# A transformer block on one core: the first Q operand on GpSimd's queue, eight more matmuls ahead of the maxima, the last K and Q parted on GpSimd, and four smaller moves

## The chip, the core and the metric

The kernel runs on one core of one Trainium2 chip. The metric is the device time of one execution in microseconds. TensorE (PE) multiplies, VectorE (DVE), ScalarE (ACT) and GpSimd (POOL) do the elementwise work, and DMAs are issued from the queues of SP, ACT and POOL. The engines run their own instructions in order and wait for each other through semaphores.

## The reference

All arrays are float32. 2048 rows of width 512 go through attention with 32 heads of 16 and a gated feed-forward part of width 1792; both are modulated by a vector `c`.

```python
mod = (_silu(c) @ w_mod).reshape(1, 6, 1, -1)
sa, ca, ga, sb, cb, gb = (mod[:, i] for i in range(6))
h = layernorm(x) * (1 + ca) + sa
q, k, v = heads(h @ wqkv)                        # 32 heads of 16
o = softmax(q @ k.T * 16 ** -0.5) @ v
x = x + ga * (merge(o) @ wo)
h = layernorm(x) * (1 + cb) + sb
x = x + gb * ((silu(h @ w_gate) * (h @ w_up)) @ w_down)
```

## The kernel before

**Numbers in two parts.** A matmul operand is held as a high part (rounded to the form that TensorE multiplies, by a cast) and a low part (what the cast left out, by a subtraction). A product takes three matmuls: high by high, high by low, low by high (`mm3`, line 205). So each operand costs a cast, mostly on ScalarE, and a subtraction, on VectorE or GpSimd.

**The ramp (lines 229 to 355).** While x and the first weights land, VectorE makes the statistics of the first 512 rows. The modulation by `sa` and `ca` is made in two halves: `mod_part` multiplies a half of `w_mod` by silu(c) into bank 7 and copies it to `ev`, `mod_col` turns it with TensorE transposes, and `half_prep` applies it to the turned rows: two casts on ScalarE, two subtractions on VectorE (line 349). In `half_prep(0, ...)` the copy of the second half's `ev` is done on VectorE (line 285, called at 347), ahead of those subtractions. `split_w` parts a block of `wqkv`: cast on ScalarE, subtraction on GpSimd (line 203).

**The projections (lines 392 to 472).** The rows are handled in four chunks of 512 (`ci`). `proj_T(ci, w, m)` gives 128 columns of Q or K, transposed: 12 matmuls into a bank, then a cast to `prt[:, 0]` (399), a subtraction out of the bank into `prt[:, 1]` (401), and two stores to the DRAM arrays `qd` and `kd` on SP's queue (404, 405). `prt` has four buffers. `proj_v` gives V for 128 rows. `Stream.jobs` writes the matmuls out one by one; every third of them advances the posts, that is, the next of the steps that follow a job. A lane is other work with a period: the lane "m" takes a step every 7 matmuls, from the second chunk on, and runs `mods()`.

**The modulation weights (lines 298 to 313 and 369 to 390).** For each of the other four sixths of `w_mod` (called 4, 3, 2 and 5) `mod_sum` multiplies four slices by silu(c) on GpSimd (line 300, one scalar operand) and adds them up (301, 302); a matmul with ones then sums over the partitions (307 for columns, 312 for rows). The weights are staged in three buffers that they share with the blocks of `wqkv`. The loads are issued on SP where `load(v)` stands: 4 and 3 at the start, 2 behind the sum of 4, 5 behind that of 3.

**The last K and Q beside the first maxima (lines 887 to 950).** The softmax needs the row maxima of the scores ahead of the scores. `max_one` (501) makes a 128 x 512 piece of scores on TensorE (line 510) and VectorE takes its maximum (512). A unit is four heads by 512 rows, with 64 such pieces in 16 steps of four; the maxima run 21 steps (`LEAD`) ahead of the scores. The generator `late` holds the projections that are left: K and Q of chunk 3, two of chunk 2, and eight of V, 216 matmuls. 22 of them come first (`take(late, 22)`); then each six maxima are followed by 14. Projections use banks in turn (`bank`), maxima others (`four`): banks 4, 5, 6 ahead of the maxima, and from there on 4 and 5, with 0, 1, 2, 3, 6, 7 for the maxima. `load_q(u)` and `load_k(u)` read a unit's Q and K from `qd` and `kd`, in two halves each; for the first three units all halves go over SP's queue, later the second halves over POOL's.

**The main loop.** Scores (line 557), exponentials (559) and the products with V (572) run unit by unit (32 of them), with maxima of the unit ahead; from the second quarter on the output projection and the feed-forward part of the finished chunk are worked in between ("filled" stretches), those without are called plain. When a unit ends, `close_unit` (894) reads the row sums back as `dn` (583), and at the steps `i0 + 3`, `+ 4`, `+ 5` come the reciprocal on VectorE (587) with its store (588), the broadcast back `rb` (593), and the multiply on GpSimd (599) with its store. `i0` is two steps behind the end, or none for a chunk's last unit. In the feed-forward part GpSimd also parts the products `mid` (832, 833), and SP loads weights (703, 708).

Of the kernel before, what the change touches and what calls it, by code (L numbers as in the profile page):

```python
# [9 lines left out]
F32 = mybir.dt.float32  # L10
# [4 lines left out]
ALU = mybir.AluOpType  # L15
# [4 lines left out]
P = 128  # L20
# [8 lines left out]
CW = S // NC  # L29
NG = H // 4  # L30
# [8 lines left out]
KR = 48  # L39
# [20 lines left out]
def take(it, k):  # L60
    run(islice(it, k))
# [40 lines left out]
def block_kernel(ctx, tc, x, wqkv, wo, w_gate, w_up, w_down, c, w_mod, out):  # L102
    nc = tc.nc
# [6 lines left out]
    sm = Stream()  # L110
# [14 lines left out]
    minus = const.tile([P, P], F32, name="minus")  # L125
    eps_t = const.tile([P, 1], F32, name="eps_t")
    one = const.tile([P, 1], F32, name="one")
    modc = const.tile([P, 4, NK], F32, name="modc")
    gb_bc = const.tile([P, D], F32, name="gb_bc")

# [141 lines left out]
        nc.tensor.matmul(banks[i % 4][:, 0:2 * P], busy[:, 0:P], busy[:, 0:2 * P], start=True, stop=True)  # L272
    nc.vector.memset(eps_t, EPS)
    nc.vector.memset(one, 1.0)
    sc = pa.tile([P, NK], F32, name="sc")
    nc.scalar.activation(sc, c_sb, AF.Silu)
    nc.scalar.activation(pa.tile([P, 1], F32, name="warm0"), eps_t, AF.Sqrt)

    def mod_part(wm, copy=nc.scalar.copy):
        pb_ = single("pmod")  # L280
        for k in range(NK):
            nc.tensor.matmul(pb_[32 * k:32 * k + 32, :], sc[:, k:k + 1].to_broadcast([P, 32]), wm[:, k, :],
                             start=True, stop=True)
        ev = pa.tile([P, D], F32, name="ev", tag="ev", bufs=1)
        copy(ev, pb_)
        return ev
# [10 lines left out]

    def mod_sum(wm):
        for k in range(NK):
            nc.gpsimd.tensor_scalar_mul(wm[:, k, :], wm[:, k, :], sc[:, k:k + 1])  # L300
        nc.gpsimd.tensor_add(wm[:, 0:2, :], wm[:, 0:2, :], wm[:, 2:4, :])
        nc.gpsimd.tensor_add(wm[:, 0, :], wm[:, 0, :], wm[:, 1, :])

# [6 lines left out]
    def sum_row(wm, dst, factor):  # L310
        pr_ = single("prow")
        nc.tensor.matmul(pr_, one.to_broadcast([P, P]), wm[:, 0, :], start=True, stop=True)
        nc.scalar.mul(dst, pr_, factor)

    def split_w(src, c0, eng=nc.gpsimd):
        cols = slice(c0, c0 + P)
        split(wqs[0][:, :, cols], wqs[1][:, :, cols], src, eng)
# [21 lines left out]
    def half_prep(ab, ev):  # L339
        mod_col(ev, half_cols(ab))  # L340
        if ab == 0:
            turn_two(2)
        tps = tps0[2 * ab:2 * ab + 2]
        lows = [modulate(pa, hT[0], tps[e], 0, 2 * ab + e, e, False) for e in range(2)]
        for _, h32, high in lows:
            nc.scalar.copy(high.bitcast(F32R), h32)
        nxt = mod_part(wm_ab[1], nc.vector.tensor_copy) if ab == 0 else None
        for low in lows:
            nc.vector.tensor_sub(*low)
        return nxt  # L350
# [1 line left out]
    bank = Turn(4, 5, 6, 7)  # L352
    turn_two(0)
    ev = half_prep(0, ev)
    split_w(wst0[:, 1], 0)

    def weights():
        st_ = {}
# [10 lines left out]
    def mods():  # L369
        def load(v):  # L370
            w = load_mod(v)
            mod_sum(w)
            return w

        def ticks(k):
            for _ in range(k):
                yield

        w4, w3 = load(4), load(3)
        yield from ticks(9)  # L380
        sum_col(w4, modc[:, 2, :], 1.0)
        w2 = load(2)
        yield from ticks(4)
        sum_col(w3, modc[:, 3, :], 0.0)
        w5 = load(5)
        yield from ticks(9)
        sum_row(w2, ga_bc, 1.0)
        yield from ticks(3)
        sum_row(w5, gb_bc, 0.5)
        yield  # L390

    def proj_T(ci, w, m, by=1):
        def job():
            pt = bank("pt")
            col = (0 if w == 0 else D) + m * P

            def post():
                prt = pa0.tile([P, 2, CW], F32R, name="prt", tag="prt", bufs=4)
                nc.scalar.copy(prt[:, 0, :], pt)  # L399
                yield  # L400
                nc.vector.tensor_sub(prt[:, 1, :], pt, prt[:, 0, :].bitcast(F32))  # L401
                yield
                dst = (qd, kd)[w][m * P:(m + 1) * P, :, ci * CW:(ci + 1) * CW]
                nc.sync.dma_start(dst[:, 1 - w:3 - w, :], prt.bitcast(F32))
# [27 lines left out]

    def load_parts(dst, src, g, c0, c1, second=nc.sync):
        heads = src[g * 64:(g + 1) * 64, :, c0:c1].rearrange("(s b d) r c -> b (d r) s c", s=2, b=2)
        for b in range(2):
            (second if b else nc.sync).dma_start(dst[64 * b:64 * b + KR].bitcast(F32), heads[b])

    def load_k0(ci):
        load_parts(kop[0][:, :, ci * CW:(ci + 1) * CW], kd, 0, ci * CW, (ci + 1) * CW)
# [56 lines left out]
    def load_q(u):  # L496
        ci, g = divmod(u, NG)
        qop[u] = pb.tile([P, 2, CW], F32R, name="qop", tag="qop", bufs=3)
        load_parts(qop[u], qd, g, ci * CW, (ci + 1) * CW, nc.gpsimd if u > 2 else nc.sync)

    def max_one(r):

# [380 lines left out]
    def hook():  # L883
        while posts:
            posts.pop(0)()

    late = sm.jobs([proj_T(last, w, m) for w, m in kq[:1] + kq[2:]] + [proj_T(last - 1, w, m) for w, m in kq[6:]] +
                   [proj_T(last, *kq[1])] + [proj_v(4 * ci + t) for ci in (last - 1, last) for t in range(4)])
    ones_rows(1)
    load_q(0)  # L890
    take(late, 22)
    load_k0(last)

    def close_unit(u, i):

        if u == NU - 1:
            res[u] = out_a(u, nc.scalar)
            return
        res[u] = out_a(u, nc.sync)
        if u + 3 < NU:  # L900
            load_k(u + 3)
            load_q(u + 3)
        i0 = i if u % NG == NG - 1 else i + 2
        at(i0 + 3, lambda: res.__setitem__(u, out_b(u, nc.sync, *res[u])))
        at(i0 + 4, lambda: res.__setitem__(u, out_r(u, nc.sync, *res[u])))
        at(i0 + 5, lambda: out_c(u, nc.gpsimd, nc.gpsimd, *res.pop(u)))
# [29 lines left out]
        if 0 <= i < UG and i % 16 in (3, 5, 8):  # L936
            next(weights2, None)

    four, bank = Turn(0, 1, 2, 3, 6, 7), Turn(4, 5)
    for i in range(-LEAD, -1):  # L940
        if i == -LEAD + 3:
            load_k(1)
# [179 lines left out]
```

## Time and profile before

| | us |
|---|---|
| median of three runs | 1861.91 |
| lowest and highest | 1861.1, 1867.45 |
| the profiled execution, and its span from first to last instruction | 1871.8, 1870.0 |
| TensorE busy | 1840.5 |
| VectorE busy | 1553.0 |
| ScalarE busy | 1243.0 |
| GpSimd busy | 455.3 |

Times in rows of the profile count from the span's start. A row of a timeline has the start, the duration, the engine with its line, the operation, what it writes and reads, and how many instructions are merged; in brackets stand the idle time ahead of it and what ended that. SPq is a DMA's issue on SP. A row of waits has the total, the number and the longest. A row of stretches has, for each engine, busy time and number of instructions, then the granted TensorE clock (1.00 is full), the DMA engines' busy share and GB/s.

### The profile page before, as it was taken

How to read it: one execution, taken by the hardware profiler on the slowest of the kernel's cores; microseconds unless marked ns; L12 is line 12 of the kernel's file. 1: busy time of each engine (PE TensorE's matmuls, PEld its weight loads, DVE VectorE, ACT ScalarE, POOL GpSimd, SP SyncE). 2: the span in 40 equal slices, each digit the busy share in tenths (PEclk: the TensorE clock that was granted, in tenths of full speed). 3: DMA queues.
4: the chain of work that ended last, by engine and by line, in shares of the span. 5: the costliest groups of instructions: out<-in, count | busy, mean ns of one | idle time of the engine just before them, and what ended most of it. 6: DMA issues, size and time to landing. Idle time of an engine off the chain costs nothing.

```text
span 1870.0 us, 41067 instructions
## 1 busy us (share of the span) xinstructions
PE 1840.5 (98%) x16904; PEld 1164.2 (62%) x16904; DVE 1553.0 (83%) x2585; ACT 1243.0 (66%) x2386; POOL 455.3 (24%) x522
## 2 busy tenths in 40 slices
PE   9989999999999999999999999999999999999998
PEld 7866444444455667666555666666554466677886
DVE  6568999989999898888999888889999988832543
ACT  4221888878887777777787776777878876674211
POOL 3710454445521311111123111111123011030200
PEclk9989999999999999999999999999999999999999
DMA  9755677766663535554364544453643445243742
GB/s 313 268 189 151 167 177 180 199 175 165 204 113 76 136 106 122 125 154 101 78 150 83 136 117 141 114 144 78 157 89 55 101 100 142 100 166 114 281 177 83
DMA packets 80584, 267.63 MB, mean 143 GB/s; under 512 B 19604, under 2 KB 24212, under 8 KB 59716
## 3 DMA queue, kind: packets, MB, share of 16 engines
q1 hardware_dynamic: 61548, 180.10, 33.1%
q0 software_dynamic: 18160, 84.10, 19.1%
q8 instruction: 133, 2.18, 0.5%
q10 hardware_dynamic: 688, 0.80, 0.1%
q14 instruction: 55, 0.45, 0.1%
HBM read 201.85 MB, written 62.13 MB: 141 GB/s over the span
## 4 chain that ended last, share of the span: by engine, by line
PE 90%; DVE 3%; DMA 3%; ACT 2%; POOL 1%; issue 0%; SPq 0%; ACTq 0%; DVEq 0%
PE bank L572 26%; PE bank L557 22%; PE bank L770 19%; PE bank L510 10%; PE bank L780 7%; PE bank L210 5%; DMA dn<-o 2%; DVE mx L512 1%; POOL wm L300 1%; DMA wm<-in_w_mod 1%; DVE stt L796 0%; PE bank L813 0%; DMA wd<-wd_dr 0%; PE bank L754 0%; DMA wm_ab<-in_w_mod 0%
## 5 line engine op out<-in xcount | busy, mean ns | idle before, releaser
L512 DVE TENSOR_REDUCE mx<-bank 128x1 f32<-128x512 f32 x2048 | 1284.2, 683 | 117.4 <-PE bank L510 86.5
L510 PE MATMUL bank<-kop,qop 48*128 48x512 f32 x2048 | 744.7, 432 | 8.7 <-DVE mx L512 4.4
L557 PE MATMUL bank<-qop,kop 50*128 50x512 f32 x2048 | 737.1, 427 | 2.6 <-ACT v_flat L427 0.2
L557 PEld LDWEIGHTS bank<-qop,kop 50*128 50x128 f32 x2048 | 344.5, 185 | 302.6 <-issue 64.7
L510 PEld LDWEIGHTS bank<-kop,qop 48*128 48x128 f32 x2048 | 342.9, 185 | 32.7 <-DVE mx L512 13.7
L770 PE MATMUL bank<-act,wgu 64*128 64x512 f32 x1872 | 296.3, 392 | 0.0
L770 PEld LDWEIGHTS bank<-act,wgu 64*128 64x128 f32 x1872 | 186.3, 187 | 31.2 <-issue 0.2
L599 POOL TENSOR_TENSOR on<-o,rb 128x512 f32<-128x512 f32 x31 | 39.7, 1281 | 446.6 <-DMA rb<-d_dr 392.2
L770 PE MATMUL bank<-wd,mid 64*128 64x512 f32 x912 | 136.4, 397 | 0.0
L832 POOL CAST mid<-m 128x512 fp32r<-128x512 f32 x40 | 24.3, 608 | 418.3 <-PE bank L510 161.3
L210 PE MATMUL bank<-hT,wqs 128*128 128x512 f32 x384 | 98.1, 408 | 6.5 <-DVE prt L401 4.2
L770 PEld LDWEIGHTS bank<-wd,mid 64*128 64x128 f32 x912 | 94.9, 185 | 11.4 <-ACT first L867 1.5
L210 PEld LDWEIGHTS bank<-hT,wqs 128*128 128x128 f32 x384 | 72.9, 194 | 28.2 <-DVE prt L401 5.5
L828 DVE SCALAR_TENSOR_TENSOR q<-th,bank 128x512 f32<-128x512 f32 x56 | 37.7, 674 | 55.2 <-ACT th L824 55.2
L824 ACT ACTIVATE th<-bank 128x512 f32<-128x512 f32 x56 | 33.2, 593 | 58.7 <-PE bank L780 58.7
L844 DVE TENSOR_TENSOR x<-bank,x 128x512 f32<-128x512 f32 x84 | 53.9, 685 | 16.7 <-PE bank L770 16.6
L399 ACT CAST prt<-bank 128x512 fp32r<-128x512 f32 x32 | 18.7, 586 | 62.4 <-PE bank L210 46.0
L830 DVE TENSOR_TENSOR m<-bank,q 128x512 f32<-128x512 f32 x56 | 38.7, 692 | 20.9 <-PE bank L780 18.8
L780 PE MATMUL bank<-wd,mid 128*128 128x512 f32 x216 | 53.3, 403 | 2.5 <-DMA wd<-wd_dr 1.9
L833 POOL TENSOR_TENSOR mid<-m,mid 128x512 fp32r<-128x512 f32 x40 | 51.6, 1289 | 3.3
L780 PEld LDWEIGHTS bank<-wd,mid 128*128 128x128 f32 x216 | 41.3, 193 | 12.7 <-ACT mid L832 2.7
L770 PE MATMUL bank<-wgu,act 64*128 64x512 f32 x288 | 48.0, 394 | 0.1
(6292 smaller groups left out, 5180.4 us busy)
## 6 DMA issues: line engine op xcount, KB each, us to landing
wgu<-gu_dr SPq DMA_DIRECT2D x48, 1024.0 KB
wd<-wd_dr SPq DMA_DIRECT2D x28, 1024.0 KB
kop<-kd SPq DMA_DIRECT2D x33, 768.0 KB
kop<-kd POOLq DMA_DIRECT2D x29, 768.0 KB, 8.6
gu_dr<-wgu POOLq DMA_DIRECT2D x14, 1024.0 KB, 14.3
kd<-prt SPq DMA_DIRECT2D x16, 512.0 KB
qd<-prt SPq DMA_DIRECT2D x16, 512.0 KB
kop<-gu_dr SPq DMA_DIRECT2D x8, 1024.0 KB
```

Of the source, the lines that this page charges most:

```text
L210: nc.tensor.matmul(pt, lhs(a, k), rhs(b, k), start=(n == 0), stop=(n == 3 * nk - 1))
L510: nc.tensor.matmul(pm, qop[u][rows, s, qt * P:(qt + 1) * P], kop[u % 3][rows, s, kc * CW:(kc + 1) * CW], start=True, stop=True)
L512: nc.vector.tensor_reduce(mx[u][:, b, s, qt, kc:kc + 1], pm, op=ALU.max, axis=AX.X)
L557: nc.tensor.matmul(sp, kop[u % 3][rows, h // 2, kt * P:(kt + 1) * P], qop[u][rows, h // 2, :], start=True, stop=True)
L572: nc.tensor.matmul(pv[u][32 * h:32 * h + 32, cols], v_flat[:, e0:e0 + 32], p_[h][:, cols], start=(kt == 0 and half == 0), stop=(kt == 15), ...
L599: mul.tensor_mul(on, o, rb)
L770: nc.tensor.matmul(outs[e], lhs(e, a, k)[rows], rhs(b, k)[rows], start=(ph == 0 and j == 0), stop=(j == z and (ph == 1 or trade is not None)),
L780: nc.tensor.matmul(outs[e], lhs(e, a, k), rhs(b, k), start=(j == 0), stop=(j == z))
L828: nc.vector.scalar_tensor_tensor(q, th, 1.0, outs[0], op0=ALU.add, op1=ALU.mult)
L830: nc.vector.tensor_mul(m32, outs[1], q)
L833: (nc.gpsimd if slow else nc.vector).tensor_sub(mid[:, 1, :], m32, mid[:, 0, :].bitcast(F32))
L844: nc.vector.tensor_add(ch.x2[:, t, :], outs[e], ch.x2[:, t, :])
```

## The change

- `half_prep(0, ...)` copies `ev` on ScalarE, and the first Q block of `wqkv` is parted on VectorE instead of GpSimd.
- `mod_sum` multiplies by silu(c) and adds a zero (`nil`), with two scalar operands in one instruction.
- `mods()` loads the weights 4, 3 and 2 at the start and 5 where 2 was; the sum of row 2 moves from the lane's step 22 to 19, that of row 5 from 25 to 28.
- All last projections of K and Q but the first go another way (`aside`): ScalarE copies the bank unrounded into `prt[:, 1]`, GpSimd casts it to `prt[:, 0]` and subtracts in place.
- Both halves of the first Q operand go over POOL's queue.
- Eight more of the late matmuls come ahead of the first maximum, and these use banks 4 and 5 alone.
- The three steps of the division come one step later, but not for a chunk's last unit.

```diff
     def mod_sum(wm):
         for k in range(NK):
-            nc.gpsimd.tensor_scalar_mul(wm[:, k, :], wm[:, k, :], sc[:, k:k + 1])
+            nc.gpsimd.tensor_scalar(wm[:, k, :], wm[:, k, :], sc[:, k:k + 1], nil[:, 0:1], op0=ALU.mult, op1=ALU.add)
...
-        nxt = mod_part(wm_ab[1], nc.vector.tensor_copy) if ab == 0 else None
+        nxt = mod_part(wm_ab[1]) if ab == 0 else None
...
-    split_w(wst0[:, 1], 0)
+    split_w(wst0[:, 1], 0, nc.vector)
...
-        w4, w3 = load(4), load(3)
+        w4, w3, w2 = load(4), load(3), load(2)
         yield from ticks(9)
         sum_col(w4, modc[:, 2, :], 1.0)
-        w2 = load(2)
+        w5 = load(5)
         yield from ticks(4)
         sum_col(w3, modc[:, 3, :], 0.0)
-        w5 = load(5)
+        yield from ticks(6)
+        sum_row(w2, ga_bc, 1.0)
         yield from ticks(9)
-        sum_row(w2, ga_bc, 1.0)
-        yield from ticks(3)
         sum_row(w5, gb_bc, 0.5)
...
-    def proj_T(ci, w, m, by=1):
+    def proj_T(ci, w, m, by=1, aside=False):
...
-                nc.scalar.copy(prt[:, 0, :], pt)
-                yield
-                nc.vector.tensor_sub(prt[:, 1, :], pt, prt[:, 0, :].bitcast(F32))
+                if aside:
+                    full = prt[:, 1, :].bitcast(F32)
+                    nc.scalar.copy(full, pt)
+                    yield
+                    nc.gpsimd.tensor_copy(prt[:, 0, :], full)
+                    nc.gpsimd.tensor_sub(prt[:, 1, :], full, prt[:, 0, :].bitcast(F32))
+                else:
+                    nc.scalar.copy(prt[:, 0, :], pt)
+                    yield
+                    nc.vector.tensor_sub(prt[:, 1, :], pt, prt[:, 0, :].bitcast(F32))
...
-        load_parts(qop[u], qd, g, ci * CW, (ci + 1) * CW, nc.gpsimd if u > 2 else nc.sync)
+        first, second = [(nc.gpsimd, nc.sync)[k] for k in ((0, 0), (1, 1), (1, 0))[min(u, 1) + (u > 2)]]
+        load_parts(qop[u], qd, g, ci * CW, (ci + 1) * CW, second, first)
...
-    late = sm.jobs([proj_T(last, w, m) for w, m in kq[:1] + kq[2:]] + [proj_T(last - 1, w, m) for w, m in kq[6:]] +
-                   [proj_T(last, *kq[1])] + [proj_v(4 * ci + t) for ci in (last - 1, last) for t in range(4)])
+    late = sm.jobs([proj_T(last, *kq[0])] + [proj_T(last, w, m, 1, True) for w, m in kq[2:]] +
+                   [proj_T(last - 1, w, m, 1, True) for w, m in kq[6:]] + [proj_T(last, *kq[1], 1, True)] + [proj_v(4 * ci + t) for ci in (last - 1, last) for t in range(4)])
     ones_rows(1)
     load_q(0)
+    four, bank = Turn(0, 1, 2, 3, 6, 7), Turn(4, 5)
     take(late, 22)
     load_k0(last)
+    take(late, 8)
...
-        i0 = i if u % NG == NG - 1 else i + 2
+        i0 = i if u % NG == NG - 1 else i + 3
...
-    four, bank = Turn(0, 1, 2, 3, 6, 7), Turn(4, 5)
```

Three places show what moves. The first is VectorE in the ramp, ahead of the second half's modulation (`ev` is its row, `hT1` the low part of the turned rows, `bank7` the bank of `mod_part`). Before:

```order
L169 TENSOR_SCALAR h32_202<-bank0_63,modc_75 128x512
L285 COPY ev_212<-bank7_70 128x512
L349 TENSOR_TENSOR hT1_148<-h32_202,hT0_147 128x512
L349 TENSOR_TENSOR hT1_148<-h32_204,hT0_147 128x512
L293 TENSOR_REDUCE cs_240<-bank7_70 128x4
```

With the change (its line numbers are a few higher):

```order
L170 TENSOR_SCALAR h32_204<-bank0_63,modc_76 128x512
L351 TENSOR_TENSOR hT1_150<-h32_204,hT0_149 128x512
L351 TENSOR_TENSOR hT1_150<-h32_206,hT0_149 128x512
L204 TENSOR_TENSOR wqs1_116<-wq0_106,wqs0_115 128x4x128
L295 TENSOR_REDUCE cs_242<-bank7_70 128x4
```

The copy is gone from ahead of the two subtractions, and the split's subtraction stands behind them. The second place is SP's queue beside the first maxima, from the rows of ones of unit 1 on (`qop_973` is the first Q operand, `kop1` unit 1's keys, `prt` the stored K or Q). Before:

```order
L491 DMA kop1_969<-kop0_87 2x4096 x2
L436 DMA qop_973<-qd_77 48x2x512 x2
L404 DMA kd_78<-prt_991 128x2x512
L405 DMA kd_78<-prt_991 128x512
L436 DMA kop0_87<-kd_78 48x2x512 x2
L404 DMA kd_78<-prt_1023 128x2x512
L405 DMA kd_78<-prt_1023 128x512
L404 DMA qd_77<-prt_1052 128x2x512
L405 DMA qd_77<-prt_1052 128x512
L436 DMA kop1_969<-kd_78 48x2x2048 x2
L436 DMA qop_1070<-qd_77 48x2x512 x2
L404 DMA kd_78<-prt_1086 128x2x512
```

With the change:

```order
L499 DMA kop1_971<-kop0_88 2x4096 x2
L412 DMA kd_79<-prt_993 128x2x512
L413 DMA kd_79<-prt_993 128x512
L444 DMA kop0_88<-kd_79 48x2x512 x2
L412 DMA kd_79<-prt_1012 128x2x512
L413 DMA kd_79<-prt_1012 128x512
L412 DMA qd_78<-prt_1043 128x2x512
L413 DMA qd_78<-prt_1043 128x512
L412 DMA kd_79<-prt_1073 128x2x512
L413 DMA kd_79<-prt_1073 128x512
L444 DMA kop1_971<-kd_79 48x2x2048 x2
L444 DMA qop_1088<-qd_78 48x2x512 x2
```

The first Q operand has left the queue, and the store of the third K block now stands ahead of unit 1's keys. The third place is GpSimd behind the sum of weight 5, where nothing stood until the main loop's loads of x and of the weights. With the change:

```order
L302 TENSOR_SCALAR wm5_672<-wm5_672,sc_145,nil_75 128x512 x4
L303 TENSOR_TENSOR wm5_672<-wm5_672 128x1024
L304 TENSOR_TENSOR wm5_672<-wm5_672 128x512
L444 DMA qop_975<-qd_78 48x2x512 x2
L404 CAST prt_1012<-prt_1012 128x512
L405 TENSOR_TENSOR prt_1012<-prt_1012 128x512
L404 CAST prt_1043<-prt_1043 128x512
L405 TENSOR_TENSOR prt_1043<-prt_1043 128x512
```

The first Q operand's two issues and nine pairs of a cast and a subtraction (two are shown) have come in there.

More of the change, by code (lines that the diff above doesn't have):

```diff
@@ L127, in block_kernel @@
     one = const.tile([P, 1], F32, name="one")
+    nil = const.tile([P, 1], F32, name="nil")
     modc = const.tile([P, 4, NK], F32, name="modc")
@@ L274, in block_kernel @@
     nc.vector.memset(one, 1.0)
+    nc.vector.memset(nil, 0.0)
     sc = pa.tile([P, NK], F32, name="sc")
@@ L430, in proj_v, with load_parts @@
         return job
-    def load_parts(dst, src, g, c0, c1, second=nc.sync):
+    def load_parts(dst, src, g, c0, c1, second=nc.sync, first=nc.sync):
         heads = src[g * 64:(g + 1) * 64, :, c0:c1].rearrange("(s b d) r c -> b (d r) s c", s=2, b=2)
         for b in range(2):
-            (second if b else nc.sync).dma_start(dst[64 * b:64 * b + KR].bitcast(F32), heads[b])
+            (second if b else first).dma_start(dst[64 * b:64 * b + KR].bitcast(F32), heads[b])
     def load_k0(ci):
```

## The prediction

> **What bounds the kernel now.** I read the busy shares first, then what TensorE waits for in the first 420 us, then the stretches around each wait.
>
> ```profile
> PE 1840.5 (98%) x16904; PEld 1164.2 (62%) x16904; DVE 1553.0 (83%) x2585; ACT 1243.0 (66%) x2386; POOL 455.3 (24%) x522
> ...
> PE bank L210 <- DVE prt L401: 5.2, 4, 1.9
> PE bank L510 <- DMA qop<-qd: 4.1, 1, 4.1
> ...
> PE bank L312 <- POOL wm L302: 1.9, 1, 1.9
> PE bank L210 <- DVE hT L349: 1.4, 1, 1.4
> ```
>
> TensorE is busy 98% of the span, so only its idle time can be won without taking work away, and the change takes no matmul away. Nearly all of that idle time lies in the front part, ahead of the first score matmul, under four names, and each edit touches one of them.
>
> ```profile
> 191.09 0.49 PE L557 MATMUL bank<-qop,kop 50*128 50x512 f32 x1
> ```
> Everything later is queued behind the front part in program order, so a microsecond won there moves the end by one, unless a later wait takes it. The stretches below give each engine's busy time and, behind them, the granted clock.
>
> ```profile
> 100.30:107.00 6.70, 6.59 (x24) 5.28 (x25) 4.12 (x7) 2.42 (x4) 0.06 (x1) 0.75 0.63 195
> 122.70:130.00 7.30, 7.30 (x22) 5.11 (x24) 4.28 (x7) 0.60 (x2) 0.00 (x0) 0.57 0.46 155
> 242.00:400.00 158.00, 157.72 (x1574) 73.85 (x1574) 156.23 (x267) 137.38 (x271) 79.14 (x81) 1.00 0.68 178
> 405.00:416.00 11.00, 8.30 (x50) 3.42 (x50) 6.04 (x11) 3.97 (x8) 0.00 (x0) 0.69 1.01 291
> ```
>
> Two readings. After three of the waits the clock is granted at 0.75, 0.57 and 0.69 for 7 to 11 us, so a wait also slows the matmuls behind it. And in the plain part of the attention (242 to 400) VectorE is busy 156.23 of 158 us: there it is VectorE that must not wait.
>
> **The ramp (VectorE and ScalarE, 13 to 21 us).**
>
> ```profile
> 15.32 0.69 DVE L285 COPY ev<-bank 128x512 f32<-128x512 f32 x1 [1.21 <-ACT hT L346]
> 15.93 2.38 DVE L349 TENSOR_TENSOR hT<-h,hT 128x512 fp32r<-128x512 f32 x2
> ...
> 21.30 1.29 DVE L349 TENSOR_TENSOR hT<-h,hT 128x512 fp32r<-128x512 f32 x2 [0.69 <-ACT hT L346]
> ...
> 15.88 1.27 POOL L203 TENSOR_TENSOR wqs<-wq,wqs 128x512 fp32r<-128x512 f32 x1 [2.93 <-ACT wqs L202]
> ...
> 21.32 17.16 PE L210 MATMUL bank<-hT,wqs 128*128 128x512 f32 x73 [0.64 <-ACT hT L346]
> ```
>
> The two subtractions that TensorE waits for come behind the copy of `ev` (0.69) and take 2.38, against 1.29 for the same pair at 21.30; GpSimd's split subtraction runs beside the slow pair. The change moves the copy to ScalarE, behind the two casts, and the split to VectorE, behind the pair. Gain: 0.69 + (2.38 - 1.29) = 1.8, and about 0.2 because the first subtraction no longer stands behind both casts: **2.0 us**. The moved split (0.65, half of 1.29) lies on VectorE while TensorE does two matmuls and four transposes, so it costs nothing; the small memset of `nil` lies ahead of the first x; without that cover it costs 0.65. Bounds 0.7 (only the copy) to 2.3. The Trainium skill, "SBUF — State Buffer", section "Who interferes with whom", says that VectorE and GpSimd lock each other out of a shared port for a whole instruction when VectorE has two SBUF inputs. The slow pair is such a case; by a rule without the lock only the 0.7 would be won.
>
> **The sums of the modulation weights (GpSimd, 53 to 100 us).**
>
> ```profile
> 80.22 6.20 POOL L300 TENSOR_SCALAR wm<-wm,sc 128x512 f32<-128x512 f32 x4 [5.86 <-DMA wm<-in_w_mod]
> 86.50 2.40 POOL L301 TENSOR_TENSOR wm<-wm 128x1024 f32<-128x1024 f32 x1
> 88.97 1.29 POOL L302 TENSOR_TENSOR wm<-wm 128x512 f32<-128x512 f32 x1
> ...
> 592.88 3.04 POOL L749 TENSOR_SCALAR mid<-x,rs,rs 128x512 f32<-128x512 f32 x4
> ...
> 100.41 1.12 PE L312 MATMUL bank<-wm,one 128*128 128x512 f32 x2 [1.85 <-POOL wm L302]
> ```
>
> One sum is 6.20 + 2.40 + 1.29 = 9.9 us; GpSimd stood 5.86 for weight 2's transfer, did its sum to 90.2, then weight 5's to 100.36, and TensorE had waited 1.85 for it. The change loads weight 2 right behind 4 and 3, and 5 where 2 stood. The form with two scalar operands is at line 749: four take 3.04, so a sum becomes 3.04 + 2.40 + 1.29 = 6.7. Weight 5 lands at about 80, its sum ends at 87 (90 if the new form costs what the old one did), and its matmul stands 28 of the lane's steps of 7 matmuls behind the start, not 25. Nothing waits in either case. Gain: 1.85, and a quarter of the 6.70 us at clock 0.75, 1.7: **3.5 us**, bounds 1.85 (the clock falls anyway) to 4.1 (all matmuls up to 107 at their usual time). The Trainium skill, "TensorE: Matmul & The Clock Gate", section "HAM oscillation — how this bites in real kernels", sets the danger at idle gaps over about 3.4 us. By that rule this gap costs 1.85 alone and the sum below would be 1.7 smaller; the trace disagrees, with 0.75 granted behind a gap of 1.85.
>
> **The first Q operand (SP, 115 to 130 us).**
>
> ```profile
> 115.03 0.36 SPq L404 DMA_DIRECT2D qd<-prt  x1
> ...
> 117.48 1.85 SPq L436 DMA_DIRECT2D qop<-qd  x2
> ...
> 122.67 1.65 PE L510 MATMUL bank<-kop,qop 48*128 48x512 f32 x6 [4.07 <-DMA qop<-qd]
> 124.25 5.70 PE L210 MATMUL bank<-hT,wqs 128*128 128x512 f32 x14
> ...
> 148.75 3.47 PE L210 MATMUL bank<-hT,wqs 128*128 128x512 f32 x14
> 152.15 0.96 PE L510 MATMUL bank<-kop,qop 48*128 48x512 f32 x6
> ```
>
> SP issues in order, so this load stood behind the stores of projections it doesn't need. On GpSimd nothing is ahead of its two issues but the sums, done by 87. Its space was weight 5's, whose matmul now stands 21 matmuls behind the place of 100.41: 100.4 + 21 x 0.24 - 5.5 (the two gains above) = about 100. TensorE needs it at 122.67 - 4.07 - 5.5 + 8 x 0.24 = 115. The wait of 4.07 goes, and with it the slow clock: 5.70 against 3.47 for fourteen matmuls and 1.65 against 0.96 for six, together 2.9. **7.0 us.** The eight matmuls are only moved: those left behind the last maxima fall from twelve to four. With two banks in turn instead of three ahead of the maxima a bank must be free twelve matmuls (2.9) after its job, and copy and subtraction (0.6 and 0.7) are done by then: nothing. Bounds: 1.9 (the load is no earlier and only the eight matmuls, 8 x 0.24, cover it) to 7.0.
>
> **K and Q of the last part (124 to 170 us).**
>
> ```profile
> 152.68 3.68 DVE L512 TENSOR_REDUCE mx<-bank 128x1 f32<-128x512 f32 x6
> ...
> 611.43 0.61 POOL L757 CAST act<-h 128x512 fp32r<-128x512 f32 x1 [11.74 <-ACT h L756]
> 612.13 1.28 POOL L758 TENSOR_TENSOR act<-h,act 128x512 fp32r<-128x512 f32 x1
> ...
> 155.05 0.59 ACT L399 CAST prt<-bank 128x512 fp32r<-128x512 f32 x1 [4.02 <-DMA kd<-prt]
> ...
> 135.64 1.52 SPq L436 DMA_DIRECT2D kop<-kd  x2
> ```
>
> Four times TensorE waited for VectorE's subtraction out of a bank, 5.2 us, since that stands behind six maxima (3.68). Now ScalarE's copy alone frees the bank. A group of 14 projections and 6 maxima takes TensorE 3.40 + 0.89 = 4.29; VectorE's six maxima take 3.6, so it keeps up; GpSimd has 0.61 + 1.28 = 1.9 per twelve matmuls, and was idle. What is late next are the four store buffers `prt`. The row at 155.05 shows a copy that waited for a buffer: the first store behind the key load of unit 1 (issued 135.64) had landed only then, 19.4 us later. In the new order that load goes out behind K2's store: K2 is done 18 late matmuls after the thirtieth, 4.4 + 2 x 0.89 = 6.2 us after the first maximum, and copy, cast, subtraction and store issue (0.59, 1.9, some 1.0) make that 9.7. The first store behind it, Q2's, then lands at 29.1; the ninth job needs its buffer, and the eleventh the bank of the ninth, at 21.9 + 7 x 0.89 = 28.1. With the copy (0.59) TensorE waits 1.6. Gain 5.2 - 1.6 = **3.6 us**, bounds 0 (the stores land 3.6 later) to 5.2.
>
> **The division one step later (from 234 us on).**
>
> ```profile
> 365.87 0.25 DVE L587 RECIPROCAL dn<-dn 128x16 f32<-128x16 f32 x1 [0.76 <-DMA dn<-o]
> ...
> 407.37 0.25 DVE L587 RECIPROCAL dn<-dn 128x16 f32<-128x16 f32 x1 [3.05 <-DMA dn<-o]
> ...
> 312.11 0.58 SPq L583 DMA_DIRECT2D dn<-o  x1
> ...
> 350.75 0.59 SPq L583 DMA_DIRECT2D dn<-o  x1
> ...
> 391.60 0.59 SPq L583 DMA_DIRECT2D dn<-o  x1
> ...
> 435.89 0.59 SPq L583 DMA_DIRECT2D dn<-o  x1
> ```
>
> A unit of 16 steps takes 350.75 - 312.11 = 38.6, so a step is 2.4 us. VectorE waited 0.76 and 3.05 for this transfer where it is the bound; one step later the waits are 0 and 0.6. The unit with the 3.05 took 435.89 - 391.60 = 44.3, 5.7 too long, since the clock was 0.69 behind it. In this execution that is worth up to 6.4. But it took 1871.8 us, 9.9 more than the median of 1861.9, and transfers that miss by so little need not miss in the others: I count half, **3 us**, bounds 0 and 6.4.
>
> **Sum**: 2.0 + 3.5 + 7.0 + 3.6 + 3 = 19.1. From the execution's own 1871.8, with the whole 6.4, it would be 1849; from the median, 1861.9 - 19.1 = **1843 us**.
>
> **Rivals.**
> - *The store buffers hold TensorE longer.* If the stores land 5 us later than 29.1, the wait is 6.6, and 3 us of clock go with it: 1843 + 8 = 1851. For it: transfers are already waited for at 155.05. Against: K2's store now goes ahead of the load.
> - *The Q load isn't earlier.* If its space comes free late, 5.1 of the 7.0 stay: 1848. Here the change wouldn't do what it says.
> - *Slower, by GpSimd's order in the feed-forward part.* The division's multiply on GpSimd comes a step later there, and the casts of `mid` stand behind it.
>
> ```profile
> 629.01 1.30 POOL L599 TENSOR_TENSOR on<-o,rb 128x512 f32<-128x512 f32 x1 [8.60 <-DMA rb<-d_dr]
> ...
> 632.14 0.61 POOL L832 CAST mid<-m 128x512 fp32r<-128x512 f32 x1 [0.92 <-DVE m L830]
> ...
> L770 PE MATMUL bank<-wd,mid x17: 384/392/448, 659.4 to 662.0; 64*128 64x512 f32 x17
> ```
>
> The cast at 632.14 had 0.92 to spare behind the multiply, less than a step, so it will be late; but its product is first read at 659.4, some 25 us on. Only where the multiply came over 25 us later would TensorE wait, in each of some 18 units; 27 us later costs 18 x 2 = 36 and gives 1843 + 36 = 1879. One step is far from that.
> - *GpSimd's new casts block VectorE's maxima.* In the ramp a VectorE pair beside GpSimd took 2.38, not 1.29. If the casts held the maxima up for their whole length, VectorE would need 3.6 + 1.9 x 14/12 = 5.8 a group against 4.29, for eight groups: 12 us back, 1855. But between 242 and 400 GpSimd was busy 79 us, and VectorE's 267 instructions took 0.59 each. The Trainium skill's lock, in the section named above, is for two SBUF inputs; the maxima read PSUM.
>
> **Chances**: forecast 0.62, store buffers 0.14, late load 0.09, blocked maxima 0.04, slower 0.06; and 0.05 that a later wait takes the front's gain (1860). The range 1836 to 1853 takes in all but the last three: up to the late load and the store buffers, and down to the upper bounds of the first, second and last terms and of the fifth by half. Half a per cent, 9.3 us, is about what a measurement of this kernel can tell: faster means under 1852.6. That is the forecast, the late load and half of the store buffers, 0.78; same 0.16; slower 0.06.
>
> **What would show it.** Right: no TensorE wait ahead of line 312's last matmul or of the first line 510; the first score near 175, not 191.1; four sums of 6.7; no subtraction out of a bank between maxima; clock 1.00 from 10 to 400. Wrong: a TensorE wait of several us near 140 with ScalarE waiting for a store, the Q load's issue after 110, or unit lengths over 38.6 in the plain part with the division's wait still there.

## The result and the profile after

| us | before | changed |
|---|---|---|
| median of 4 runs | 1861.51 | 1845.6 |
| lowest, highest | 1860.89, 1867.45 | 1845.14, 1845.71 |
| profiled execution, span | 1871.8, 1870.0 | 1845.7, 1843.9 |

The ratio is 0.9907, 95% interval 0.9887 to 0.9927. The medians are 15.9 us apart, 0.9%; the forecast was 18.9. A second set, taken with the experiments, has 1847.49 against 1863.44, again 15.9 between the medians, ratio 0.9923 (0.9908 to 0.9938). The sign and the range held; the 1843 itself was 2.6 too low.

The page of the changed kernel first, its span, TensorE's busy time and the row of the granted clock:

```profile
span 1843.9 us, 41081 instructions
...
PE 1829.7 (99%) x16904; PEld 1155.2 (63%) x16904; DVE 1538.7 (83%) x2577; ACT 1243.2 (67%) x2387; POOL 460.7 (25%) x541
...
PEclk9999999999999999999999999999999999999999
```

The two profiled executions are 26.1 us apart in span. TensorE's busy time fell by 10.8 between them (1840.5 to 1829.7) for the same 16904 matmuls, so that part of the 26.1 is clock and not waiting. What TensorE still waits for in the changed kernel, longest total first (total, times, longest):

```profile
PE bank L519 <- DVE mx L521: 1.9, 6, 0.3
PE bank L284 <- DMA wm_ab<-in_w_mod: 1.2, 2, 0.8
...
PE bank L211 <- ACT hT L348: 0.6, 1, 0.6
PE bank L211 <- ACT v_flat L435: 0.6, 1, 0.6
PE bank L211 <- ACT prt L402: 0.6, 1, 0.6
```

None of the waits that the change was to remove is left; the row for `prt` is the store buffers, priced at 1.6. GpSimd's own row of time shows the new sum of weight 5, then the first Q load, then the first parted projection:

```profile
78.91 3.28 POOL L302 TENSOR_SCALAR wm<-wm,sc,nil 128x512 f32<-128x512 f32 x4 [2.47 <-DMA wm<-in_w_mod]
82.27 2.40 POOL L303 TENSOR_TENSOR wm<-wm 128x1024 f32<-128x1024 f32 x1
84.75 1.29 POOL L304 TENSOR_TENSOR wm<-wm 128x512 f32<-128x512 f32 x1
104.95 1.39 POOL L444 DMA_DIRECT2D qop<-qd  x2 [18.91 <-PE bank L314]
114.72 0.61 POOL L404 CAST prt<-prt 128x512 fp32r<-128x512 f32 x1 [8.38 <-ACT prt L402]
115.42 1.28 POOL L405 TENSOR_TENSOR prt<-prt 128x512 fp32r<-128x512 f32 x1
```

And TensorE at the same places: the end of the ramp, weight 5's matmul, the first maximum, the two waits that are left, the first score (line 566).

```profile
19.79 5.39 PE L211 MATMUL bank<-hT,wqs 128*128 128x512 f32 x21 [0.65 <-ACT hT L348]
...
103.62 1.02 PE L314 MATMUL bank<-wm,one 128*128 128x512 f32 x2
104.08 11.26 PE L211 MATMUL bank<-hT,wqs 128*128 128x512 f32 x47
115.27 0.96 PE L519 MATMUL bank<-kop,qop 48*128 48x512 f32 x6
116.16 3.47 PE L211 MATMUL bank<-hT,wqs 128*128 128x512 f32 x14
...
144.13 2.11 PE L211 MATMUL bank<-wqs,hT 128*128 128x512 f32 x8 [0.57 <-ACT prt L402]
...
163.09 1.18 PE L211 MATMUL bank<-wqs,hT 128*128 128x512 f32 x4 [0.58 <-ACT v_flat L435]
...
174.41 0.49 PE L566 MATMUL bank<-qop,kop 50*128 50x512 f32 x1
```

The first score stands at 174.41, 16.7 before its old place (191.09). Fourteen projection matmuls take 3.47 from the first maximum on, where they took 5.70. The two profiled executions part by another 9.4 behind the first score (1678.9 us to the end before, 1669.5 after), but the one before was 10 us above its median, and the medians part by only 15.9 in all. By these two traces alone, then, the front gives everything, and the later division nothing. That was my **first theory**; its **rival** was the prediction's own term, 3 us for the division.

### The profile page after: what moved, and what is told of

Its sections match the earlier page's. It is cut to its first block, busy times and chain, and to the rows that moved or that the text cites. A ratio compares the mean times of both kernels' runs of the same rounds, so it can differ in the third digit from the quotient of the medians.

```text
span 1843.9 us, 41081 instructions
## 1 busy us (share of the span) xinstructions
PE 1829.7 (99%) x16904; PEld 1155.2 (63%) x16904; DVE 1538.7 (83%) x2577; ACT 1243.2 (67%) x2387; POOL 460.7 (25%) x541
## 4 chain that ended last, share of the span: by engine, by line
PE 94%; DVE 2%; DMA 2%; ACT 2%; SPq 0%; issue 0%; POOL 0%; ACTq 0%; DVEq 0%; POOLq 0%
PE bank L581 27%; PE bank L566 23%; PE bank L779 19%; PE bank L519 9%; PE bank L789 7%; PE bank L211 6%; DVE mx L521 1%; DMA qd<-prt 1%; PE bank L822 1%; DVE stt L805 1%; DMA wm_ab<-in_w_mod 0%; PE bank L763 0%; DMA qop<-mr 0%; PE bank L531 0%; PE bank L163 0%
## 5 line engine op out<-in xcount | busy, mean ns | idle before, releaser
L211 PE MATMUL bank<-hT,wqs 128*128 128x512 f32 x384 | 93.4, 396 | 0.7 <-ACT hT L348 0.6
L211 PEld LDWEIGHTS bank<-hT,wqs 128*128 128x128 f32 x384 | 70.8, 188 | 19.5 <-issue 2.7
L211 PE MATMUL bank<-wqs,hT 128*128 128x512 f32 x192 | 47.5, 398 | 1.1 <-ACT v_flat L435 0.6
```

The source lines that it names most:

```text
L211: nc.tensor.matmul(pt, lhs(a, k), rhs(b, k), start=(n == 0), stop=(n == 3 * nk - 1))
```

## The experiments

Each time is a median, beside the kernel before on the same chip; the difference in us is the ratio's, with its 95% interval. Three dots in a code cut stand for lines left out.

### The division

The step alone, on the kernel before:

```diff
-        i0 = i if u % NG == NG - 1 else i + 2
+        i0 = i if u % NG == NG - 1 else i + 3
```

> The kernel before with the division one step later and nothing else. First theory (all of the 15.9 us comes from the front, each removed wait with the slow clock behind it, and the division's waits of 0.76 and 3.05 belong to single executions): 1861.5 within 1 us, no change. Rival (the prediction's own term: half of 6.4 us is there in the usual execution, and the front is worth 3 less than the trace says): 1858.5, 3.0 us faster.

Measured: 1860.74 against 1863.84, 2.2 us faster (0.2 to 4.3), between no change and the rival's 3.0. The reverse, `i + 2` in the changed kernel:

> The changed kernel with the division put back to its old step. First theory: as the changed kernel, 1845.6, or up to 0.8 us faster, since the front alone then explains 16.7 of 15.9 us. Rival (the division's step is worth 3 us): 1848.6, 3 us slower than the changed kernel, 12.9 us under the kernel before.

Measured: 1849.22 (1845.66 to 1852.02) against 1863.84, 14.5 faster than before (11.4 to 17.7). That lies between the two theories (15.9 or more, and 12.9) and decides nothing. And `i + 1` in the kernel before:

> The kernel before with the division one step (2.4 us) earlier instead of later. From issue to reading there are then 12.0 us instead of 14.4. First theory (the transfer usually lands well ahead of its reading): within 3 us of the kernel before. Rival (the transfer lands close to 14.4 us in every execution, so the margin of the kernel before is thin and the term of 3 us is real): VectorE waits 1 to 3 us in most of the about 15 units of the plain part, and the kernel is 10 to 30 us slower.

Measured: 1864.12 against 1863.84, 1.7 us slower (0.2 faster to 3.4 slower), as the first theory had it. Here are VectorE's reciprocals of the fourth and the fifth unit. One step earlier:

```profile
362.15 0.25 DVE L587 RECIPROCAL dn<-dn 128x16 f32<-128x16 f32 x1 [0.32 <-DMA dn<-o]
403.39 0.25 DVE L587 RECIPROCAL dn<-dn 128x16 f32<-128x16 f32 x1 [2.80 <-DMA dn<-o]
```

The kernel before with the step later:

```profile
369.43 0.24 DVE L587 RECIPROCAL dn<-dn 128x16 f32<-128x16 f32 x1
409.59 0.24 DVE L587 RECIPROCAL dn<-dn 128x16 f32<-128x16 f32 x1
```

The same two units wait, and with less room they don't wait longer (0.76 and 3.05 before), so the transfer doesn't land close to its reading everywhere, as this run's rival had it; it is late in two units, by an amount that changes from one execution to the next. With the step later neither waits. Why these two are late is open: in the kernel before the DMA engines were 1.01 to 1.04 busy from issue to reading in them, and in three units around them that don't wait. Two more runs were to show the step against its absence on one chip:

> The changed kernel once more, beside the others of this group. Theory now (every execution without the later division has VectorE waits for it in the fourth to sixth unit, so the step is worth 2 to 4 us, and the front 17): 18 to 21 us under the kernel before of the same chip, times within 1 us of each other. Rival (the step is worth nothing): 16 us under it.

Measured: 1847.49 (1846.08 to 1851.8), 14.3 faster than before (11.6 to 17.1) and 15.9 between the medians. The theory's 18 to 21 missed; the rival's 16 held.

> The changed kernel with the division at its old step, beside the changed kernel on one chip. Theory now: 2 to 4 us slower than the changed kernel, in most executions a slow stretch of the clock behind a wait near 390 us, and times that scatter over 5 us. Rival: the same time as the changed kernel within 1 us.

Measured: 1848.37 (1846.02 to 1850.87), 14.5 faster (12.1 to 17.0). That is 0.9 above the changed kernel where the theory had 2 to 4; the rival held here too. But the wait is there, in the fourth unit and the fifth:

```profile
352.17 0.25 DVE L596 RECIPROCAL dn<-dn 128x16 f32<-128x16 f32 x1 [1.43 <-DMA dn<-o]
391.44 0.25 DVE L596 RECIPROCAL dn<-dn 128x16 f32<-128x16 f32 x1 [0.81 <-DMA dn<-o]
```

The changed kernel, from its first trace, has none:

```profile
350.18 0.24 DVE L596 RECIPROCAL dn<-dn 128x16 f32<-128x16 f32 x1
390.33 0.24 DVE L596 RECIPROCAL dn<-dn 128x16 f32<-128x16 f32 x1
```

So the first theory falls as it stood: the step does remove a wait. In the five traces with the later step neither unit waits, in each of the nine others at least one does. From the fourth issue of `dn` to the seventh, three units take 116.9 to 117.2 us in the five traces with the later step, and 117.8 to 123.8, 120.4 on average, in the eight with the old one: 3.4 us. But in time the step alone gave 2.2, and taking it away cost 0.9 between medians and nothing by the ratios. The scatter of the clock hides it: with the slow clock taken off each time (the last table of the next section), the step is worth 1.8 us alone and 1.5 taken out, 1.0 either way.

One such wait is left. The eighth unit is a chunk's last, whose step the change leaves as it was. VectorE waited there for the same transfer in two of the five traces with the later step, 0.97 us in the second trace of the changed kernel and 2.10 in one of the runs below (the old form of the multiplication), and behind the 2.10 the clock was at half for 6.83 us.

### The sums of the modulation weights

The new load order and the two-scalar form alone, on the kernel before (both parts as in the diff above):

```diff
+    nil = const.tile([P, 1], F32, name="nil")
...
-            nc.gpsimd.tensor_scalar_mul(wm[:, k, :], wm[:, k, :], sc[:, k:k + 1])
+            nc.gpsimd.tensor_scalar(wm[:, k, :], wm[:, k, :], sc[:, k:k + 1], nil[:, 0:1], op0=ALU.mult, op1=ALU.add)
...
-        w4, w3 = load(4), load(3)
+        w4, w3, w2 = load(4), load(3), load(2)
...
-        w2 = load(2)
+        w5 = load(5)
...
-        w5 = load(5)
+        yield from ticks(6)
+        sum_row(w2, ga_bc, 1.0)
         yield from ticks(9)
-        sum_row(w2, ga_bc, 1.0)
-        yield from ticks(3)
         sum_row(w5, gb_bc, 0.5)
```

> The kernel before with the new order of the weight loads and the two-scalar form of the sums, nothing else. First theory (a wait of 1.85 us costs its length and the slow clock behind it): 3.5 us faster, 1858.0, no wait ahead of the second matmul of line 312's last sum, four sums of about 7.0 us, clock 1.00 around 100 us. Rival (the clock falls there whatever the wait): 1.85 us faster, 1859.7, with a slow stretch of about 3.4 us near 100 us all the same. In both the wait of the first score for its Q operand stays, 4.1 us.

Measured: 1861.41 against 1863.84, 2.6 us faster (0.4 to 5.0), between the two. TensorE no longer waits at line 312 (314 in this kernel), and the clock stayed at 1.00 there. Then the changed kernel with the old form of the multiplication, the order kept:

```diff
-    nil = const.tile([P, 1], F32, name="nil")
...
-            nc.gpsimd.tensor_scalar(wm[:, k, :], wm[:, k, :], sc[:, k:k + 1], nil[:, 0:1], op0=ALU.mult, op1=ALU.add)
+            nc.gpsimd.tensor_scalar_mul(wm[:, k, :], wm[:, k, :], sc[:, k:k + 1])
```

> The changed kernel with the old one-scalar form of GpSimd's multiplications. Theory (the earlier load of weight 2 alone hides the sums, as the prediction says: weight 5's sum then ends at about 90 and is read at 104): as the changed kernel within 1 us, no wait ahead of line 312's matmuls. Rival (the form is needed): a wait of some us there and the slow clock behind it, 2 to 5 us slower than the changed kernel.

Measured: 1848.9 beside 1847.49 for the changed kernel on this chip, 1.4 more where the theory allowed 1, and without the wait that the rival expected; against before 13.6 faster (11.4 to 16.0), where the changed kernel has 14.3 (11.6 to 17.1). GpSimd's last sum in that run:

```profile
86.17 6.20 POOL L300 TENSOR_SCALAR wm<-wm,sc 128x512 f32<-128x512 f32 x4
92.45 2.40 POOL L301 TENSOR_TENSOR wm<-wm 128x1024 f32<-128x1024 f32 x1
94.93 1.36 POOL L302 TENSOR_TENSOR wm<-wm 128x512 f32<-128x512 f32 x1
105.23 1.39 POOL L442 DMA_DIRECT2D qop<-qd  x2 [8.95 <-PE bank L312]
```

It ends at 96.3 and is read at 103.9. The new order of the loads is enough; in it the form halves the multiplications (6.20 to 3.28) in time that nobody waits for. The new form with the old order was not run.

### The first Q operand and the eight matmuls

On the kernel before, the queue alone, the eight matmuls alone, and both:

```diff
-    def load_parts(dst, src, g, c0, c1, second=nc.sync):
+    def load_parts(dst, src, g, c0, c1, second=nc.sync, first=nc.sync):
...
-            (second if b else nc.sync).dma_start(dst[64 * b:64 * b + KR].bitcast(F32), heads[b])
+            (second if b else first).dma_start(dst[64 * b:64 * b + KR].bitcast(F32), heads[b])
...
-        load_parts(qop[u], qd, g, ci * CW, (ci + 1) * CW, nc.gpsimd if u > 2 else nc.sync)
+        first, second = [(nc.gpsimd, nc.sync)[k] for k in ((0, 0), (1, 1), (1, 0))[min(u, 1) + (u > 2)]]
+        load_parts(qop[u], qd, g, ci * CW, (ci + 1) * CW, second, first)
```

> The kernel before with the first Q operand issued from GpSimd instead of SP, nothing else. Theory (the issue follows the last matmul of weight 5 at about 101 and lands some 12 us later, before it is needed at 118.6; the wait of 4.07 goes with 2.9 us of slow clock): first maximum at about 118.6 and 7 us faster than the kernel before. Rival (only the length of the wait is won, the clock falls behind the other waits): 4 us faster. Second rival (its space is free too late): 0 to 2 us.

```diff
+    four, bank = Turn(0, 1, 2, 3, 6, 7), Turn(4, 5)
     take(late, 22)
     load_k0(last)
+    take(late, 8)
...
-    four, bank = Turn(0, 1, 2, 3, 6, 7), Turn(4, 5)
```

> The kernel before with the eight late matmuls moved ahead of the maxima, nothing else. Theory: they cover 1.9 of the wait of 4.07; about 2.1 are left and the clock still falls behind them: 1 to 3 us faster than the kernel before. Rival (the eight are what removes the wait): 5 to 7 us faster.

> Both of the last two edits on the kernel before. Theory (the queue alone already removes the wait): as the kernel with the queue alone within 1 us, about 7 us faster than the kernel before. Rival (each needs the other): 3 us or more faster than the kernel with the queue alone.

Measured against 1864.04: the queue alone 1859.89, 5.0 us faster (3.0 to 7.1); the eight alone 1863.49, 0.4 faster (from 1.9 slower to 2.6 faster); both 1857.25, 5.8 faster (3.4 to 8.2). The queue does most of it. The eight alone came out below the 1 to 3 of their theory, and beside the queue they add 0.8 by the ratios and 2.6 between the medians (the theory allowed 1, the rival had 3 or more), which these times can't tell from nothing. With the queue alone the first maximum waits for nothing, and yet 5.0 came and not the theory's 7. TensorE in that run:

```profile
117.51 0.96 PE L511 MATMUL bank<-kop,qop 48*128 48x512 f32 x6
118.40 3.47 PE L210 MATMUL bank<-hT,wqs 128*128 128x512 f32 x14
...
138.17 2.01 PE L210 MATMUL bank<-hT,wqs 128*128 128x512 f32 x6 [1.86 <-DVE prt L401]
140.12 1.65 PE L511 MATMUL bank<-kop,qop 48*128 48x512 f32 x6
141.69 5.54 PE L210 MATMUL bank<-hT,wqs 128*128 128x512 f32 x14
```

Fourteen matmuls take 5.54 again, now behind the third wait for VectorE's subtraction. That wait has the same 1.86 in the kernel before, and there the clock stayed up. The expectation's first rival, that the clock falls behind the other waits, was right for this execution.

### K and Q of the last part

The copies by ScalarE and the split by GpSimd alone, on the kernel before:

```diff
-                nc.scalar.copy(prt[:, 0, :], pt)
-                yield
-                nc.vector.tensor_sub(prt[:, 1, :], pt, prt[:, 0, :].bitcast(F32))
+                if aside:
+                    full = prt[:, 1, :].bitcast(F32)
+                    nc.scalar.copy(full, pt)
+                    yield
+                    nc.gpsimd.tensor_copy(prt[:, 0, :], full)
+                    nc.gpsimd.tensor_sub(prt[:, 1, :], full, prt[:, 0, :].bitcast(F32))
+                else:
...
```

> The kernel before with the late K and Q projections copied by ScalarE and split by GpSimd, nothing else. Theory: the four waits for VectorE's subtraction (5.2 us) go, and a store-buffer wait of 0.5 to 1.6 comes: 3.6 to 4.7 us faster than the kernel before. Rival (the stores land later, since K2's store isn't ahead of the key load here): 0 to 2 us faster, with ScalarE's copy waiting for a store.

Measured: 1856.7 against 1864.04, 6.9 us faster (4.7 to 8.9), more than the theory's 3.6 to 4.7. TensorE's one wait there for a store buffer:

```profile
151.56 0.73 PE L210 MATMUL bank<-hT,wqs 128*128 128x512 f32 x2
152.79 3.00 PE L210 MATMUL bank<-hT,wqs 128*128 128x512 f32 x12 [0.50 <-ACT prt L401]
```

The same edit taken out of the changed kernel:

> The changed kernel with the late K and Q projections split by VectorE out of the bank again, as before. Theory (the term of K and Q, 4.4 us by the two traces): 4 to 5 us slower than the changed kernel, four waits of TensorE for VectorE's subtraction, 5.2 us in all, between the first maximum and the first score. Rival (with the earlier Q and the eight matmuls the subtractions are no longer late, or the clock drops behind their waits): 0 to 1 us, or over 8 us.

Measured: 1854.46 (1849.32 to 1860.75), 7.0 above the changed kernel's 1847.49 and 8.6 below before (5.8 to 11.4). TensorE waits for VectorE again:

```profile
PE bank L211 <- DVE prt L402: 4.2, 3, 1.9
```

Three waits and not four, and the same 4.2 us, are also in both runs with the eight moved matmuls. In the profiled execution the first score comes 4.2 us after that of the changed kernel (178.62 against 174.41), as the theory has it. The nine runs lose more and scatter over 11 us, and the granted clock with them, from 1.0 in one of 1851.23 us to 0.994 in the one of 1860.75.

## Why the prediction was right, and where its sum was too large

| term | predicted | shown |
|---|---|---|
| ramp | 2.0 | 2.0 in four traces, 1.5 in two |
| sums | 3.5 | 2.6 alone (0.4 to 5.0) |
| first Q operand, eight matmuls | 7.0 | 5.8 alone (3.4 to 8.2) |
| K and Q of the last part | 3.6 | 6.9 alone (4.7 to 8.9), 7.0 between medians when taken out |
| division | 3 | 2.2 alone (0.2 to 4.3), 0.9 between medians when taken out |
| together | 19.1 | 15.9, twice; ratios 17.3 (13.6 to 21.0) and 14.3 (11.6 to 17.1) |

**The ramp** came as worked out. From the start of the last matmul with `wm_ab` to the end of TensorE's wait for ScalarE's casts of the second half it was 6.7 us in all eight traces with the old code, and 4.7 in four of the six with the new (5.2 in the other two). The pair of subtractions ahead of it takes 1.29, where it took 2.38 with GpSimd beside it:

```profile
15.34 1.29 DVE L351 TENSOR_TENSOR hT<-h,hT 128x512 fp32r<-128x512 f32 x2 [0.69 <-ACT hT L348]
16.87 0.69 DVE L204 TENSOR_TENSOR wqs<-wq,wqs 128x512 fp32r<-128x512 f32 x1 [0.23 <-ACT wqs L203]
```

In each of the eight old traces one of the two subtractions takes 1.76 to 1.79, in the six new ones each takes 0.69 at most. This agrees with the lock of the Trainium skill, "SBUF — State Buffer", section "Who interferes with whom". The ramp was not run by itself.

**The sums**: weight 5's ended at 86.04, predicted 87, in 7.0 us instead of 6.7. The wait went. The working's "90 if the new form costs what the old one did" was short, since the four old sums then run one behind the other: 96.3, still ahead of its reading. The mis-sized part is the 1.7 of clock. In the seven traces that keep the wait, it is 1.40 to 2.13 us, 1.77 on average, and only in two did the clock fall behind it.

**The first Q operand**: issued at 104.95 (predicted 100), needed at 115.27 (predicted 115), in time. The 100 left out 16 transposes that stand among the 21 matmuls (about 1.6 us), and took off the 1.7 of slow clock, which lay behind that place and not ahead of it. The 4.07 went. Its clock, 2.9, is near what that wait costs: in all six traces that keep it, at 1.96 to 4.07 us, the clock is at half behind it, for 3.41 or 6.83 us (up to 1.7 or 3.4 lost). But with the queue alone the clock fell behind another wait instead.

**K and Q**: the mechanism was right and the size too small. The store buffers held TensorE for 0.57 where 1.6 was predicted, and for 0.17 to 0.97 in the other five traces with this edit. ScalarE's copy waited for a store as foreseen; it began 28.2 us after the first maximum, where the landing was put at 29.1:

```profile
143.49 0.59 ACT L402 COPY prt<-bank 128x512 f32<-128x512 f32 x1 [6.94 <-DMA qd<-prt]
```

The 0.58 for V's copy at 163.09 belongs to the eight matmuls and their two banks, which the prediction put at nothing: 0.58 to 0.66 in all eight traces with them, and in none of the others. They also take away one of the four waits for VectorE. The traces make K and Q worth 4.2 to 4.7; why the edit alone gave more in the timed runs is open.

**The division** was counted at half of what one execution showed, 6.4, and that execution was the worst of eight (123.8 us for the three units, 120.4 on average). The 3 lies inside the interval of the run alone (0.2 to 4.3).

**The rivals.** GpSimd's feed-forward order and blocked maxima did not come. TensorE's wait for `mid` was 0.4 in all before and 0.3 after, and VectorE's six maxima take 3.68 beside the new casts, as before:

```profile
120.09 3.68 DVE L521 TENSOR_REDUCE mx<-bank 128x1 f32<-128x512 f32 x6 [0.54 <-PE bank L519]
```

One reading was off without harm to the sum: of TensorE's 29.5 us of idle time in the kernel before, 15.3 lie ahead of the first score, and 12.6 of these under the four names. That is half and not nearly all.

How the front's time is made up can be checked. From the start of the last matmul with `wm_ab` to the first score, with the time at half clock in it, in us of the profiled executions:

| kernel | stretch | half clock in it |
|---|---|---|
| before | 176.5 | 10.2 |
| division alone | 176.3 | 10.2 |
| division earlier | 173.9 | 6.8 |
| sums alone | 171.5 | 3.4 |
| Q queue alone | 170.7 | 6.8 |
| eight alone | 171.0 | 3.4 |
| queue and eight | 167.8 | 0 |
| K and Q alone | 167.5 | 3.4 |
| changed, without K and Q | 163.6 | 0 |
| changed | 159.4 | 0 |

Take the queue alone: 176.5, less the wait of 4.07, less half of the 3.4 us that no longer run at half clock, is 170.7, and the trace has 170.7. For the changed kernel, the ramp's 2.0, 1.85, 4.07, the 5.2 of VectorE less 1.15 of new waits, and 5.1 of clock: 159.4, as in the trace. In all fourteen traces the stretch less its ramp, its waits and half of its time at half clock is 153.1 to 154.1 us. So in the front a wait costs its length. The clock behind it is another matter: it fell behind two of seven waits for the sums (1.40 to 2.13), behind one of eight of VectorE's third (1.86), and behind six of six for the first Q operand. The prediction took the clock of one execution as the price of each wait; the three traces with the front of before have 6.8 to 10.2 us at half clock, worth 3.4 to 5.1.

The mean granted clock is known for every run, with or without a profile. What it lacks to 1, times the span, is an estimate of the time lost to it (three digits, so good to 0.9 us in one run): 5.9 to 6.8 us on average in the kernel before. With it, the difference of the means can be parted, in us faster than before on the same chip, with 95% intervals:

| kernel | in all | of it clock | the rest |
|---|---|---|---|
| division alone | 2.0 | 0.2 ± 1.4 | 1.8 ± 1.0 |
| division one step earlier | -0.8 | -1.7 ± 1.4 | 0.9 ± 1.2 |
| sums alone | 2.2 | 0.7 ± 1.5 | 1.5 ± 1.0 |
| Q queue alone | 5.1 | 0.7 ± 2.3 | 4.4 ± 1.1 |
| eight alone | 0.6 | -1.4 ± 1.7 | 2.0 ± 1.1 |
| queue and eight | 6.2 | 2.7 ± 2.2 | 3.4 ± 1.2 |
| K and Q alone | 7.3 | 0.9 ± 1.6 | 6.4 ± 1.4 |
| changed, without K and Q | 8.7 | 1.3 ± 2.6 | 7.4 ± 0.9 |
| changed, division at its old step, first run | 14.8 | 3.2 ± 3.0 | 11.5 ± 2.1 |
| the same, beside the changed kernel | 14.7 | 4.0 ± 2.2 | 10.7 ± 0.9 |
| changed, old form of the sums | 13.8 | 0.3 ± 1.7 | 13.5 ± 1.1 |
| changed | 14.6 | 2.5 ± 2.8 | 12.2 ± 0.9 |

The rest is close to the lengths of the waits: 1.5 for 1.85, 4.4 for 4.07, 2.0 for the 1.9 that eight matmuls cover. Of the predicted 19.1, about 13 are waits and 6 are clock. The changed kernel has 12.2 of the one and 2.5 of the other, so the step that was too large is the clock, as far as its wide interval can tell. K and Q were too small, 3.6 against 4.8 (the changed kernel without it against with it) to 6.4. That the total came within 3 us is in part luck, since these two errors partly offset each other. The single edits add up to 19.5 with the ramp, some 4 us either way, and the whole is 15.9: whether they overlap isn't shown.

## What to carry to other kernels

Price a wait at its length, and the slow clock behind it as a chance, here two in seven and one in eight for waits of 1.40 to 2.13 us, six in six for those of 1.96 to 4.07: take it over several executions, or give it as a range. Where the clock scatters by more than the edit is worth, take the time lost to each run's granted clock off before comparing. A late transfer that one trace shows at one place needs more traces before its size is counted; here the same wait was 0 to 3.05 us. Where a load stands behind stores it doesn't need, moving it to an idle queue was worth more (4.4) than work moved ahead of it (2.0).

## What was not expected of the hardware

**The clock changes on a grid of 3.41 us.** Within each of the fourteen traces every stretch at half clock starts a whole multiple of 3.41 us from the others and, unless the execution ends first, lasts 3.4, 6.8 or once 13.7. In the front it goes with how much of the 3.41 us ahead of it TensorE stood idle. Stretches of the kernel before, cut on that grid (columns as before; the clock is the number behind POOL):

```profile
98.32:101.73 3.41, 1.56 (x6) 0.80 (x5) 3.38 (x4) 0.16 (x1) 1.96 (x2) 1.00 0.07 26
101.73:105.14 3.41, 3.41 (x14) 2.95 (x13) 2.13 (x4) 1.64 (x3) 0.00 (x0) 0.50 0.79 250
...
142.69:146.10 3.41, 1.71 (x8) 1.07 (x6) 3.41 (x6) 0.59 (x1) 0.00 (x0) 1.00 0.99 144
146.10:149.52 3.42, 3.26 (x15) 2.21 (x16) 1.84 (x4) 0.00 (x0) 0.00 (x0) 1.00 0.93 129
```

And of the kernel with the queue alone:

```profile
98.36:101.77 3.41, 1.67 (x8) 0.92 (x6) 3.41 (x4) 0.00 (x0) 2.54 (x2) 1.00 0.28 103
101.77:105.18 3.41, 3.41 (x19) 2.71 (x18) 2.64 (x5) 1.71 (x3) 1.40 (x2) 1.00 0.60 201
135.91:139.32 3.41, 1.55 (x7) 0.95 (x6) 2.81 (x5) 0.59 (x1) 0.00 (x0) 1.00 1.09 147
139.32:146.15 6.83, 6.83 (x20) 4.46 (x19) 4.37 (x7) 0.59 (x1) 0.00 (x0) 0.50 0.97 258
```

Busy for 1.56 or 1.55 of 3.41, and the next stretch runs at 0.50; busy for 1.67 or 1.71, and it doesn't. The wait for VectorE is 1.86 long in both kernels: in the one it falls across two stretches, in the other inside one. Between 30 and 200 us, in all fourteen traces, eleven stretches at full clock had TensorE idle for 1.85 us or more, and behind nine of them the clock was halved; of those idle for 0.55 to 1.75, behind none. The two exceptions (idle 1.92 and 1.85) are unexplained. Ahead of 30 us it was four of five, idle for 1.98 to 2.53. In the scores and maxima behind them less is enough, 0.77 in one trace. The Trainium skill, "TensorE: Matmul & The Clock Gate", section "What's actually happening", describes such a window of 3413 ns that runs free of the kernel's start, and the traces agree; its rule of the section "HAM oscillation — how this bites in real kernels", that the danger begins with gaps over about 3.4 us, they contradict: 1.85 inside one window was enough.

**Some half-clock stretches have no wait ahead of them**: 13.65 us from 189.49 with the eight matmuls alone, 3.41 at 1402 in the kernel before. That is open. The runs of one kernel scatter with their clock: of fourteen runs of the kernel before, beside the changed one, the two with 0.999 granted took 1859.0 and 1859.66 us, the one with 0.995 took 1866.35.
